# A gated scan with a mixture of experts: blank rows and row loads on all DMA rings, late jobs in whole tiles and rests, and new durations in the planner

## The chip, the core and the metric

The kernel runs on one core of a Trainium2 chip. A core has a matrix engine (PE; its weight loads are listed apart as PEld), a vector engine (DVE), an activation engine (ACT), POOL and SP, and 16 DMA engines that all queues share. Here SP issues the plain DMAs and POOL the indexed ones. The metric is the device time of one execution in microseconds; the median of three runs before the change is 884.57 us.

## The reference

Two stages, in float32. First a gated scan along each of four sequences of 3648 steps with 256 channels, then a mixture of 4 x 4 experts on the 14592 rows that come out:

```python
sig = 1.0 / (1.0 + np.exp(-f_logit))
f = lower_bound + (1.0 - lower_bound) * sig
for t in range(S):
    h = f[:, t] * h + (1 - f[:, t]) * x[:, t]
    y[:, t] = h
...
g_idx = argmax(y @ w_group)              # a group of four experts for each row
e_idx = argmax(y @ w_expert[g_idx])      # one expert in the group
out[row] = g_w * e_w * (np.maximum(y[row] @ w1[g, e], 0.0) @ w2[g, e])
```

`g_w` and `e_w` are the softmax weights of the chosen group and expert. An expert has a 256 x 1024 and a 1024 x 256 matrix.

## The kernel before, in words

**Front.** The rows are handled in 29 units of 512 (the last is half a unit), two units to a group. For a unit SP loads gates and inputs (`zt`, 1 MB, four buffers), ACT computes the gate (L352, L357), DVE the inflow and the scan of both channel halves (L362, L378). PE turns the result back to rows (L386) and computes the router's logits in four column groups (L401). For a group DVE finds each row's expert and its place in that expert's region of a scratch tensor `xs` in memory (the lines from L431 to L505), and POOL scatters the rows there, 128 to a DMA (L520).

**Expert jobs.** An expert's rows are worked off in two jobs. Its early job (kind A) takes the first n x 128 rows as soon as a certain unit is routed: `EARLY` has (unit, n) for each expert. When all rows are routed, DVE sorts the experts by what is left (`order`), and the late jobs (kind B) take the sorted experts one by one, with room for `CAPS[s]` rows at rank s. What fits no room would go through a loop at the end; with the data at hand it has no turn, before and after the change. Since an early job may start with fewer rows than it takes, each expert's region is preceded by rows that are blank, with an index that sends their result nowhere; a common block of blank rows serves jobs that have to be skipped. `blanks` (L322) writes them.

**A job.** SP loads four quarters of an expert's weights (`st`, 512 KB each, five buffers, L706) and the rows (`xr`, up to 256 rows to a piece, six buffers, L691). ACT rounds weights to float16 (L711), DVE puts the remainder in bfloat16 (L714). PE turns the rows (L732), ACT and DVE split them in the same way (L744, L748). The first product (L770 to L772, three partial products) has the weights as the stationary side and a chunk of two or three tiles of rows as the moving side; ACT applies the maximum with 0 (L787), DVE takes the remainder (L791). The second product (L803 to L805) has a tile's hidden rows as the stationary side and moves 256 columns of weights, 24 products to a tile; ACT scales the result (L816), and POOL scatters it to the output (L821). Three halves of PSUM banks take the second product's results in turn.

**The order.** `Plan` is a list scheduler that runs when the kernel is built. Each piece of work has an engine, a duration, what it depends on, the buffers it takes and a due time; a DMA has a size and goes through a model of shared bandwidth. The planner plays the program through with these numbers and writes out one fixed order for each engine. On the chip an engine runs its list in order and waits by semaphores. So a duration in the table changes the order of instructions, not the instructions. The due times are laid out from `BEGIN`, the time at which the first job is put.

Of the kernel before, what the change touches and what calls it, by code (L numbers as in the profile page):

```python
# [14 lines left out]
I32 = mybir.dt.int32  # L15
# [31 lines left out]
class Plan:  # L47
# [23 lines left out]
    def order(self):  # L71
# [44 lines left out]
        def rates():  # L116
            act = [e for e, q in queues.items() if q]
            return {e: min(380.0, 400.0 / len(act)) for e in act}

        def advance(now):  # L120
            left = now - clock[0]
            clock[0] = now
            for e, r in rates().items():
                b = left * r
                q = queues[e]
                while q and b > 0:
                    g = min(b, q[0][1])
                    q[0][1] -= g
                    b -= g
                    if q[0][1] <= 1e-3:  # L130
                        push(now + 900.0, finish, q.popleft()[0])
# [60 lines left out]
def gated_scan_moe(ctx: ExitStack, tc, zx, lower, wroute, wexp, out, S):  # L192
# [9 lines left out]
    BLK = P * max(t for t, _ in CAPS + [(n, P) for _, n in EARLY])  # L202
# [76 lines left out]
    for s in range(NE):  # L279
        V.memset(caps[:, s:s + 1], float(CAPS[s][0] * CAPS[s][1]))  # L280
# [41 lines left out]
    def blanks():  # L322
        b = rt.tile([P, 4, RW], F32, name="rows", bufs=ROW_BUFS)
        k = 4
        b = b.bitcast(I32)
        nc.gpsimd.memset(b, 0)
        nc.gpsimd.memset(b[:, :, D:D + 1], N)
        b = b.rearrange("p k c -> p (k c)")
        for r in range(0, BLK, P * k):
            n = min(P, (BLK - r) // k)  # L330
            sync.dma_start(out=xs_v[NT][r:r + n * k, :].rearrange("(p k) c -> p (k c)", k=k), in_=b[0:n])
        for q in range(0, NE, k):
            at = xs_v[NT + 1][FIRST - P + q * PITCH:FIRST - P + q * PITCH + 1, :]
            sync.dma_start(out=bass.AP(at.tensor, at.offset, [[PITCH * RW, k], [k * RW, P // k], [1, k * RW]]), in_=b)
# [308 lines left out]
    def make_job(kind, idx):  # L643
        j = Job()
        j.kind, j.idx = kind, idx
        j.tiles, j.w = (EARLY[idx][1], P) if kind == "A" else CAPS[idx] if kind == "B" else (1, P)
# [7 lines left out]
        j.pieces = [(c + t, min(2, m - t)) for c, m in j.chunks for t in range(0, m, 2)]  # L654
        j.cols = []
        for _, m in j.chunks:
            n = UNIT // (m * j.w)
# [18 lines left out]
    def piece_mask(j, pi):  # L676
        t0, m = j.pieces[pi]
        mk = j.mask[pi] = mo.tile([P, 2], I32, name="mk", bufs=16)
        if j.kind == "B":
            V.tensor_scalar(out=mk[:, 0:m], in0=rowno[m], scalar1=float(t0 * j.w),  # L680
# [4 lines left out]
    def job_rows(j):  # L685
        job_e(j)
        word = j.pos if j.kind == "A" else regs["pordi"][0:1, j.idx:j.idx + 1] if j.kind == "B" else regs["tabs"][0:1, 1:2]
        pos = sync.value_load(word, min_val=0, max_val=LROWS - j.tiles * j.w)
        for pi, (t0, m) in enumerate(j.pieces):
            r = j.rows[pi] = mo.tile([P, 2, RW], I32, name="xr", bufs=XR_BUFS)  # L690
            ld = sync.dma_start(out=r[0:j.w, 0:m],  # L691
                                in_=xs[bass.ds(pos + t0 * j.w, m * j.w), :].rearrange("(p k) c -> p k c", k=m))
# [26 lines left out]
    def x_turn(j, pi):  # L719
# [9 lines left out]
        p = j.w  # L729
# [5 lines left out]
    def x_views(j, pi):  # L735
        t0, m = j.pieces[pi]
        ch = chunk_of(j, t0)
        lo, w = (t0 - j.chunks[ch][0]) * j.w, m * j.w
# [35 lines left out]
    def m1_views(j, ch, cs):  # L774
        w = j.chunks[ch][1] * j.w
# [17 lines left out]
    def m2_mm(j, ch, t):  # L793
        p = j.w
        pm = j.pm[ch, t, "y"] = y_slot()
        ts = slice(t * p, (t + 1) * p)
        for c in range(KF):
            if j.full:
                nc.tensor.matmul(pm[0:p], j.hh[ch][:, c, ts], j.wh[2 + c // 4][:, (c % 4) * D:(c % 4 + 1) * D],
                                 start=(c == 0), stop=(c == KF - 1))  # L800
                continue
            wh, wl = (q[2 + c // 4][:, (c % 4) * D:(c % 4 + 1) * D] for q in (j.wh, j.wl))
            nc.tensor.matmul(pm[0:p], j.hh[ch][:, c, ts], wh, start=(c == 0), stop=False)  # L803
            nc.tensor.matmul(pm[0:p], j.hh[ch][:, c, ts], wl, start=False, stop=False)  # L804
            nc.tensor.matmul(pm[0:p], j.hl[ch][:, c, ts], wh, start=False, stop=(c == KF - 1))  # L805
# [6 lines left out]
    def m2_scale(j, ch, t):  # L812
        p = j.w
# [3 lines left out]

    def m2_out(j, ch, t):
        p = j.w
# [10 lines left out]
    def m1_ns(j, ch):  # L830
        return KF * KD * (4 if j.full else 3) * (j.chunks[ch][1] * j.w / 2.4 + 2.4)

    def m2_ns(j):
        return KF * (4 if j.full else 3) * 109.0
# [3 lines left out]
    for j in jobs:  # L838
        j.s1, j.s2 = {}, {}
        for ch in range(len(j.chunks)):  # L840
# [4 lines left out]
            if tail is not None:  # L845
                tj, tch = tail
                for t in range(tj.chunks[tch][1]):
                    tj.s2[tch, t] = clock
                    clock += m2_ns(tj)
            tail = (j, ch)  # L850
    tj, tch = tail
    for t in range(tj.chunks[tch][1]):
        tj.s2[tch, t] = clock
        clock += m2_ns(tj)

    want = {}
# [22 lines left out]
    for g, G in groups.items():  # L879
# [4 lines left out]
        for u in G["units"]:  # L884
            w = unit_range(u)[1] - unit_range(u)[0]
            q = w / 512.0
            k0 = key - 9000.0
# [16 lines left out]
            else:  # L904
                ld = A("SP", 340, lambda u=u: load_unit(u), key=k0 - 6000.0, new=[zt], size=int(1050000 * q))
# [13 lines left out]
            r = A("PE", 460, lambda u=u: router(u), after=sc, key=k0 + 1000, use=[hb], new=[("p", u, "r")])  # L919
# [4 lines left out]
        k1 = key - 6000.0  # L924
        rr, lg = ("rt", g), ("Lg", g)
        mx = A("DVE", 100 + 440 * frac, lambda g=g: route_max(g), after=lgs, key=k1, use=[lg], new=[rr])
        ex = A("ACT", 90 + 140 * frac, lambda g=g: route_exp(g), after=[mx], key=k1 + 100, use=[rr])
        fi = A("DVE", 150 + 600 * frac, lambda g=g: route_first(g), after=[mx], key=k1 + 200, use=[rr])
        ct = A("DVE", 150 + 480 * frac, lambda g=g: route_count(g), after=[fi], key=k1 + 300, use=[rr])
# [6 lines left out]
        ix = A("DVE", 100 + 520 * frac, lambda g=g: route_index(g), after=[pl], key=k1 + 600, use=[rr])  # L936
        tk = A("ACT", 130, lambda g=g: route_token(g), after=[mx], key=k1 + 150, use=[rr])
        wt = A("DVE", 250 + 380 * frac, lambda g=g: route_weight(g), after=[ex, fi, tk], key=k1 + 700, use=[rr])
# [3 lines left out]
        if g in close_at:  # L942
            T1[g] = A("DVE", 300 * len(runs(close_at[g])), lambda g=g: close(g), after=[tot], key=k1 + 800)
            ends[g] = [T1[g]]
        sct = [A("POOL", 1280, lambda g=g, t=t: scatter(g, t), after=[ix, pays[t // 4], copies[t // 2]], key=key - 4000.0 + t,
                 use=[rr, ("rows", G["units"][t // 4])], size=135000) for t in range(T)]
# [3 lines left out]
    tables = A("DVE", 2500, leftovers, after=[put], key=jobs[-13].at)  # L950
    regs["left"] = None

    for n, j in enumerate(jobs):
        base = j.at
        dep = [T1[member[EARLY[j.idx][0]]]] if j.kind == "A" else [put]
        rows_dep = dep + groups[member[EARLY[j.idx][0]] if j.kind == "A" else last]["scattered"]
# [4 lines left out]
        for i in range(4):  # L961
            d = base - 3000.0 + 700.0 * i if i < 2 else j.s2[0, 0] - 4000.0 + 1300.0 * (i - 2)
            ld = A("SP", 370, lambda j=j, i=i: job_weights(j, i), after=wdep, key=d - 9000.0,
# [8 lines left out]
        ld = A("SP", 500 + 370 * np_, lambda j=j: job_rows(j), after=rows_dep, key=base - 9500.0, new=xr, size=int(265000 * j.tiles * j.w / 256))  # L972
# [118 lines left out]
```

## Time and profile before

| what | value |
|---|---|
| median of 3 runs | 884.57 us (882.73 to 887.25) |
| the profiled execution's own time | 880.72 us |
| its span | 879.0 us |
| mean granted PE clock | 0.965 |
| PE / DVE / ACT / POOL busy | 753.7 / 537.3 / 463.5 / 294.2 us |
| moved by DMA | 146.89 MB |

An engine's busy time says how long instructions of it were in work; what sets the end is read from the idle time of the engine that is nearly always busy, and from what ended it. A row of a wait reads: who waited, for whom, how many microseconds in total, how often, the longest. A row of a stretch has its bounds, its length, and for PE, PEld, DVE, ACT and POOL the busy time and the number of instructions, then the granted PE clock, the mean busy share of the DMA engines, and GB/s.

### The profile page before, as it was taken

Reading aid. Unit: us, or ns where it says so; the run is one execution under the profiler, and the core shown is the slowest. Engines: PE = TensorE matmul, PEld = TensorE weight load, DVE = VectorE, ACT = ScalarE, POOL = GpSimd, SP = SyncE. Lnnn points to the kernel's source line nnn. Section 1 sums busy time; section 2 is a strip of 40 time slices with the busy share of each in tenths; the row PEclk is TensorE's granted clock in tenths of the full one; section 3 lists DMA queues with packets and bytes.
Section 4 is the critical chain, followed back from the end, with each engine's and each line's share of the span. In section 5 each row is a group of like instructions: output and inputs, shape, how many; then the busy total and the mean of one; then the engine's idle time right before and its main releaser. Section 6 shows DMA issues by size and latency. Waiting matters only on the chain.

```text
span 879.0 us, 17343 instructions
## 1 busy us (share of the span) xinstructions
PE 753.7 (86%) x6667; PEld 646.3 (74%) x6667; DVE 537.3 (61%) x1067; ACT 463.5 (53%) x852; POOL 294.2 (33%) x255
## 2 busy tenths in 40 slices
PE   3513499879897998998997698999999999999995
PEld 2312287767586787786886587999889989999894
DVE  6917999888895975753458452553654534655460
ACT  6506788666775764453434352543554544545551
POOL 0553726175425435515122121322321312222121
PEclk9999699988999999999999799999999999999998
DMA  7595888778856654314007641423543434443320
GB/s 288 168 326 208 298 326 297 251 232 303 277 202 220 211 188 150 123 59 141 23 31 234 215 117 46 158 73 111 156 143 103 122 105 136 144 153 122 108 95 19
DMA packets 48192, 146.89 MB, mean 167 GB/s; under 512 B 10707, under 2 KB 12958, under 8 KB 44652
## 3 DMA queue, kind: packets, MB, share of 16 engines
q1 hardware_dynamic: 33579, 115.67, 40.3%
q0 software_dynamic: 14240, 30.06, 10.0%
q8 instruction: 53, 0.87, 0.4%
q14 instruction: 32, 0.25, 0.1%
q10 hardware_dynamic: 288, 0.03, 0.0%
HBM read 112.65 MB, written 33.60 MB: 166 GB/s over the span
## 4 chain that ended last, share of the span: by engine, by line
PE 64%; DVE 8%; DMA 7%; issue 5%; ACT 2%; POOL 1%; another core or an unknown queue 1%; POOLq 0%; DVEq 0%; ACTq 0%
PE ps_y L803 10%; PE ps_y L805 10%; PE ps_y L804 10%; PE ps_m L770 10%; PE ps_m L772 10%; PE ps_m L771 10%; DMA st<-in_wexp_dram 4%; DMA xr<-xs 2%; DVE w L714 2%; PE ps_p L386 2%; DVE hh L791 2%; PE ps_p L732 2%; PE ps_p L401 1%; POOL out_dram L821 1%; ACT w L711 1%
## 5 line engine op out<-in xcount | busy, mean ns | idle before, releaser
L821 POOL DMA_INDIRECT out_dram<-o,meta x123 | 149.1, 1212 | 447.3 <-ACT o L816 412.2
L803 PE MATMUL ps_y<-w,hh 128*128 128x256 f16 (+6 forms) x984 | 269.9, 274 | 11.8 <-ACT o L816 10.2
L805 PE MATMUL ps_y<-w,hh 128*128 128x256 f16 (+6 forms) x984 | 269.8, 274 | 0.6 <-issue 0.6
L804 PE MATMUL ps_y<-w,hh 128*128 128x256 bf16 (+6 forms) x984 | 269.8, 274 | 0.0
L770 PE MATMUL ps_m<-x,w 128*128 128x256 f16 (+12 forms) x896 | 252.4, 283 | 10.4 <-DVE hh L791 8.2
L771 PE MATMUL ps_m<-x,w 128*128 128x256 bf16 (+12 forms) x896 | 252.4, 283 | 8.0 <-DVE x L748 5.5
L772 PE MATMUL ps_m<-x,w 128*128 128x256 f16 (+12 forms) x896 | 252.2, 282 | 0.3 <-issue 0.3
L791 DVE SCALAR_TENSOR_TENSOR hh<-ps_m,hh 128x512 bf16<-128x512 f32 (+11 forms) x270 | 164.2, 620 | 134.3 <-ACT hh L787 120.1
L787 ACT ACTIVATE hh<-ps_m 128x512 f16<-128x512 f32 (+11 forms) x270 | 146.0, 546 | 125.2 <-PE ps_m L772 109.1
L714 DVE TENSOR_TENSOR w<-st,w 128x1024 bf16<-128x1024 f32 x128 | 154.0, 1218 | 77.1 <-ACT w L711 74.9
L520 POOL DMA_INDIRECT xs<-rows,posi x114 | 142.3, 1248 | 128.2 <-issue 39.5
L816 ACT ACTIVATE o<-ps_y,meta 128x256 f32<-128x256 f32 (+6 forms) x123 | 57.1, 473 | 193.7 <-PE ps_y L805 147.2
L711 ACT CAST w<-st 128x1024 f16<-128x1024 f32 x128 | 132.6, 1049 | 20.0 <-DMA st<-in_wexp_dram 20.0
L804 PEld LDWEIGHTS <-hh 128*128 128x128 f16 (+6 forms) x984 | 111.5, 113 | 18.6 <-issue 11.5
L803 PEld LDWEIGHTS <-hh 128*128 128x128 f16 (+6 forms) x984 | 111.5, 113 | 9.6 <-issue 2.3
L805 PEld LDWEIGHTS <-hh 128*128 128x128 bf16 (+6 forms) x984 | 111.5, 113 | 8.0 <-issue 1.1
L771 PEld LDWEIGHTS <-w 128*128 128x128 f16 x896 | 88.7, 99 | 30.1 <-issue 14.4
L772 PEld LDWEIGHTS <-w 128*128 128x128 bf16 x896 | 88.7, 99 | 27.4 <-issue 11.2
L770 PEld LDWEIGHTS <-w 128*128 128x128 f16 x896 | 88.8, 99 | 18.4 <-issue 3.4
L378 DVE TENSOR_TENSOR_SCAN h<-zt,h 128x512 f32<-128x512 f32 (+4 forms) x56 | 65.4, 1172 | 0.9 <-PE ps_p L386 0.9
L401 PE MATMUL ps_p<-h,wr 128*32 128x128 f32 x456 | 26.5, 337 | 40.5 <-DVE h L378 27.3
L748 DVE TENSOR_TENSOR x<-ps_p,x 128x512 bf16<-128x512 f32 (+9 forms) x68 | 39.7, 613 | 20.8 <-ACT x L744 20.7
(126 smaller groups left out, 508.0 us busy)
## 6 DMA issues: line engine op xcount, KB each, us to landing
st<-in_wexp_dram SPq DMA_DIRECT2D x128, 512.0 KB
zt<-in_zx_dram SPq DMA_DIRECT2D x27, 1024.0 KB
xr<-xs SPq DMA_DIRECT2D x31, 258.0 KB
xs<-rows SPq DMA_DIRECT2D x5, 516.0 KB
xr<-xs SPq DMA_DIRECT2D x8, 249.9 KB
out_dram<-o,meta POOLq DMA_INDIRECT x123
xs<-rows,posi POOLq DMA_INDIRECT x114
xr<-xs SPq DMA_DIRECT2D x6, 241.9 KB
```

The lines of the kernel that those rows point to most:

```text
L520: sc = nc.gpsimd.indirect_dma_start(out=xs_v[G["t0"] + t][:, :], out_offset=bass.IndirectOffsetOnAxis(ap=G["posi"][:, t:t + 1], axis=0), i ...
L711: nc.scalar.copy(j.wh[i], j.st[i])
L714: V.tensor_tensor(out=j.wl[i], in0=j.st[i], in1=j.wh[i], op=ALU.subtract)
L770: nc.tensor.matmul(po, wh, xh[:, k], start=(k == 0), stop=False)
L771: nc.tensor.matmul(po, wh, xl[:, k], start=False, stop=False)
L772: nc.tensor.matmul(po, wl, xh[:, k], start=False, stop=(k == KD - 1))
L787: nc.scalar.activation(hi, pv, AF.Relu)
L791: V.scalar_tensor_tensor(out=lo, in0=pv, scalar=0.0, in1=hi, op0=ALU.max, op1=ALU.subtract)
L803: nc.tensor.matmul(pm[0:p], j.hh[ch][:, c, ts], wh, start=(c == 0), stop=False)
L804: nc.tensor.matmul(pm[0:p], j.hh[ch][:, c, ts], wl, start=False, stop=False)
L805: nc.tensor.matmul(pm[0:p], j.hl[ch][:, c, ts], wh, start=False, stop=(c == KF - 1))
L821: last_out[0] = nc.gpsimd.indirect_dma_start(out=out_v[out_n[0]][:, :], out_offset=bass.IndirectOffsetOnAxis(ap=lt[0:p, r, 0:1], axis=0), ...
```

## The change

**Blanks.** One constant tile of 64 x 2 blank rows is filled once by POOL. The region leads are written for four experts in one DMA, the common block in pieces, all with an outer dimension of 64, and each just ahead of the early jobs that need it. Before, all were written in one step, planned at 25 us, and the DMA of four leads had an outer dimension of 4.

**Late jobs.** `CAPS` is now a number of rows, a multiple of 32. A job is cut into whole tiles of 128 rows and, where needed, a rest of 64 and a rest of 32. Before, a late job was n tiles of one width, 92 to 128 rows. A chunk of the first product may now be up to 384 rows of mixed tiles. For a rest the second product splits the hidden dimension in two or four parts, which go to column groups of 64 or 32 of the matrix engine and to different partitions of PSUM; ACT scales the first part and DVE adds the others (`m2_sum`).

**Numbers.** Two early jobs are smaller by one tile each, one of them starts a unit earlier. `BEGIN` goes from 55 to 85 us, weights may be loaded 16 us ahead instead of 20, the bandwidth is 340 GB/s in all, a landing takes 1.5 us, and many durations of the planner's table are replaced. The core of the diff:

```diff
-         (14, 3), (16, 4), (18, 4), (20, 4), (22, 5), (24, 5), (26, 6), (26, 6)]
-CAPS = [(7, 124), (6, 128), (6, 124), (5, 124), (5, 120), (5, 116), (5, 108), (4, 128),
-        (4, 120), (4, 120), (4, 116), (4, 108), (3, 128), (3, 104), (2, 92), (1, 128)]
+         (14, 3), (16, 4), (18, 4), (20, 4), (22, 4), (23, 5), (26, 6), (26, 5)]
+CAPS = [864, 768, 736, 608, 608, 576, 544, 512, 480, 480, 448, 448, 448, 416, 288, 128]
-BEGIN = 55.0
-BLANKS_AT = 25000.0
+BEGIN = 85.0
-AHEAD = 20000.0
+AHEAD = 16000.0
+RATE = 340.0
+LAND = 1500.0
+POOL_NS = 1400.0
...
-            return {e: min(380.0, 400.0 / len(act)) for e in act}
+            return {e: RATE / len(act) for e in act}
...
-        for q in range(0, NE, k):
-            at = xs_v[NT + 1][FIRST - P + q * PITCH:FIRST - P + q * PITCH + 1, :]
-            sync.dma_start(out=bass.AP(at.tensor, at.offset, [[PITCH * RW, k], [k * RW, P // k], [1, k * RW]]), in_=b)
+    def blank_common(r, n):
+        sync.dma_start(out=xs_v[NT][r:r + n * P, :].rearrange("(n p k) c -> p n (k c)", p=P // 2, k=2),
+                       in_=blank.rearrange("p k c -> p (k c)")[:, None, :].broadcast_to([P // 2, n, 2 * RW]))
+
+    def blank_leads(e, n):
+        at = xs_v[NT + 1][FIRST - P + e * PITCH:FIRST - P + e * PITCH + 1, :]
+        sync.dma_start(out=bass.AP(at.tensor, at.offset, [[2 * RW, P // 2], [PITCH * RW, n], [1, 2 * RW]]),
+                       in_=blank.rearrange("p k c -> p (k c)")[:, None, :].broadcast_to([P // 2, n, 2 * RW]))
...
+        j.tw = [P] * (j.cap // P)
+        for w in (64, 32):
+            if sum(j.tw) + w <= j.cap:
+                j.tw.append(w)
...
-            m = 3 if j.tiles - t == 3 else min(2, j.tiles - t)
+            m = j.tiles - t if sum(j.tw[t:]) <= 3 * P else 2
...
+        parts = P // p
+        n = KF // parts
+        for i in range(n):
...
+            for m in range(len(prods[0])):
+                for q in range(parts):
+                    c = q * n + i
+                    h, w = prods[q][m]
+                    nc.tensor.matmul(pm[q * p:(q + 1) * p], h[:, c, ts], w[2 + c // 4][:, (c % 4) * D:(c % 4 + 1) * D],
+                                     start=(i == 0 and m == 0), stop=(i == n - 1 and m == len(prods[0]) - 1),
+                                     **({"tile_position": (0, q * p)} if parts > 1 else {}))
...
+    def m2_sum(j, ch, t):
...
+        for q in range(1, P // p):
+            V.scalar_tensor_tensor(out=o[0:p], in0=j.pm[ch, t, "y"][q * p:(q + 1) * p], scalar=lt.bitcast(F32)[0:p, r, 1:2],
+                                   in1=o[0:p], op0=ALU.mult, op1=ALU.add)
...
-    def m2_ns(j):
-        return KF * (4 if j.full else 3) * 109.0
+    def m2_ns(j, ch, t):
+        return KF * (4 if j.full else 3) * 109.0 * j.tw[j.chunks[ch][0] + t] / P
...
-            r = A("PE", 460, lambda u=u: router(u), after=sc, key=k0 + 1000, use=[hb], new=[("p", u, "r")])
+            r = A("PE", 1050, lambda u=u: router(u), after=sc, key=k0 + 1000, use=[hb], new=[("p", u, "r")])
...
-    A("SP", 1100, blanks, after=[], key=0.0, new=[("rows", "blank")], size=3000000, wait=BLANKS_AT)
-    put = A("DVE", 4200, order, after=[tot, *T1.values()], key=need[last] - 3000.0, new=[("h", "order")])
+    put = A("DVE", 6000, order, after=[tot, *T1.values()], key=need[last] - 3000.0, new=[("h", "order")])
```

More of the change, by code (lines that the diff above doesn't have):

```diff
@@ L320, in unit_range, with blank_rows @@
         return u * UNIT, min(N, (u + 1) * UNIT)
[L322 to L331, printed above, removed]
-        for q in range(0, NE, k):
-            at = xs_v[NT + 1][FIRST - P + q * PITCH:FIRST - P + q * PITCH + 1, :]
-            sync.dma_start(out=bass.AP(at.tensor, at.offset, [[PITCH * RW, k], [k * RW, P // k], [1, k * RW]]), in_=b)
+    blank = const.tile([P // 2, 2, RW], I32, name="blank")
+    def blank_rows():
+        nc.gpsimd.memset(blank, 0)
+        nc.gpsimd.memset(blank[:, :, D:D + 1], N)
+    def blank_common(r, n):
[5 more added lines that the diff above has]
+                       in_=blank.rearrange("p k c -> p (k c)")[:, None, :].broadcast_to([P // 2, n, 2 * RW]))
     def load_unit(u, k=None):
@@ L650, in make_job @@
         while t < j.tiles:
[L651 removed]
+            m = j.tiles - t if sum(j.tw[t:]) <= 3 * P else 2
             j.chunks.append((t, m))
             t += m
[L654 removed]
+        j.cw = [j.to[t + m] - j.to[t] for t, m in j.chunks]
+        j.pieces = []
+        for c, m in j.chunks:
+            t = c
+            while t < c + m:
+                n = 2 if t + 1 < c + m and j.tw[t] == j.tw[t + 1] == P else 1
+                j.pieces.append((t, n))
+                t += n
         j.cols = []
[L656 to L657 removed]
+        for w in j.cw:
+            n = UNIT // w
             j.cols.append([list(range(c, min(KF, c + n))) for c in range(0, KF, n)])
@@ L942, in gated_scan_moe, with blanked @@
         if g in close_at:
-            T1[g] = A("DVE", 300 * len(runs(close_at[g])), lambda g=g: close(g), after=[tot], key=k1 + 800)
+            T1[g] = A("DVE", 390 * len(runs(close_at[g])), lambda g=g: close(g), after=[tot], key=k1 + 800)
             ends[g] = [T1[g]]
-        sct = [A("POOL", 1280, lambda g=g, t=t: scatter(g, t), after=[ix, pays[t // 4], copies[t // 2]], key=key - 4000.0 + t,
+        sct = [A("POOL", POOL_NS, lambda g=g, t=t: scatter(g, t), after=[ix, pays[t // 4], copies[t // 2]], key=key - L_SCATTER + t,
                  use=[rr, ("rows", G["units"][t // 4])], size=135000) for t in range(T)]
         G["scattered"] = (groups[g - 1]["scattered"] if g else []) + sct
-    A("SP", 1100, blanks, after=[], key=0.0, new=[("rows", "blank")], size=3000000, wait=BLANKS_AT)
-    put = A("DVE", 4200, order, after=[tot, *T1.values()], key=need[last] - 3000.0, new=[("h", "order")])
-    tables = A("DVE", 2500, leftovers, after=[put], key=jobs[-13].at)
+    made = A("POOL", 900, blank_rows, key=0.0, wait=3000.0)
+    late = need[last] - 25000.0
+    leads = {}
+    for q in range(0, NE, 4):
+        at = min([j.at for j in jobs if j.kind == "A" and q <= j.idx < q + 4] + [late])
+        leads[q] = A("SP", 340, lambda e=q: blank_leads(e, 4), after=[made], key=at - 17000.0, size=540000, wait=at - 30000.0)
+    commons = []
+    done = 0
+    for j in jobs:
+        n = j.tiles if j.kind == "A" else BLK // P
+        if n > done:
+            at = min(j.at, late)
+            commons.append((n, A("SP", 340, lambda a=done * P, n=n - done: blank_common(a, n), after=[made], key=at - 16500.0,
+                                 size=132000 * (n - done), wait=at - 30000.0)))
+            done = n
+    def blanked(j):
+        n = j.tiles if j.kind == "A" else BLK // P
+        return ([leads[j.idx // 4 * 4]] if j.kind == "A" else list(leads.values())) + [t for m, t in commons if m <= n]
+    put = A("DVE", 6000, order, after=[tot, *T1.values()], key=need[last] - 3000.0, new=[("h", "order")])
+    tables = A("DVE", 3500, leftovers, after=[put], key=jobs[-13].at)
     regs["left"] = None
```

123 lines of the change are left out of this document (71 added, 52 removed).

## The prediction

> **What bounds the kernel now.** I read the page's head first, then busy time in six stretches (the columns are the length, then PE, PEld, DVE, ACT and POOL busy, granted clock, DMA share and GB/s).
>
> ```profile
> span 879.0 us, 17343 instructions
> PE 753.7 (86%) x6667; PEld 646.3 (74%) x6667; DVE 537.3 (61%) x1067; ACT 463.5 (53%) x852; POOL 294.2 (33%) x255
> 0.00:109.00 109.00, 40.89 (x298) 26.01 (x299) 74.63 (x185) 61.11 (x115) 48.43 (x54) 0.92 0.73 257
> 109.00:340.00 231.00, 210.60 (x1899) 172.52 (x1899) 191.33 (x336) 159.51 (x292) 107.94 (x85) 0.96 0.72 246
> 340.00:473.00 133.00, 123.06 (x1073) 101.62 (x1072) 73.26 (x188) 56.76 (x119) 47.27 (x45) 0.99 0.30 96
> 473.00:543.00 70.00, 55.64 (x449) 47.05 (x449) 35.87 (x77) 28.80 (x48) 10.56 (x8) 0.90 0.51 156
> 543.00:863.00 320.00, 318.36 (x2907) 294.48 (x2906) 162.21 (x285) 156.01 (x277) 76.62 (x61) 1.00 0.39 119
> 863.00:879.00 16.00, 5.15 (x48) 4.61 (x45) 0.00 (x0) 1.30 (x3) 3.38 (x3) 0.80 0.07 18
> ```
>
> PE idles 68.1 us before the first expert product at 109, 20.4 in the next stretch, 9.9, then 14.4 where the late jobs begin, and only 1.6 in 543 to 863. So the end is PE's work plus those idle times: after 543 only less PE work helps, before it only shorter waits. Two waits stand out. The first, from the waits of 24 to 75 us and then SP's rows and the busy time in slices:
>
> ```profile
> DVE mx L431 <- ACT Lg L420: 25.1, 3, 24.2
> ACT zt L352 <- DMA zt<-in_zx_dram: 23.1, 2, 22.9
> PE ps_p L412 <- ACT rs L407: 20.9, 1, 20.9
> 30.67 8.81 SPq L334 DMA_DIRECT2D xs<-rows  x4
> 39.59 8.81 SPq L344 DMA_DIRECT2D zt<-in_zx_dram  x2
> 36.00:40.00 4.00, 1.69 (x15) 1.11 (x13) 3.69 (x7) 1.73 (x5) 3.39 (x3) 1.00 0.37 98
> 52.00:56.00 4.00, 0.00 (x0) 0.00 (x0) 0.00 (x0) 0.00 (x0) 2.92 (x3) 1.00 1.01 397
> ```
>
> Four blank stores go out at 30.7; while they run the DMA engines are 0.37 busy at 98 GB/s, against 397 GB/s later, and the next load of zx lands so late that ACT waits 22.9 us, DVE 24.2 behind it, PE 20.9 behind both. Nothing else works then: this is the whole front, stopped.
>
> The second wait, where the late jobs start (waits of 474 to 500, the row loads' own view, two slices):
>
> ```profile
> ACT w L711 <- DMA st<-in_wexp_dram: 11.8, 3, 11.2
> PE ps_y L803 <- ACT o L816: 9.7, 1, 9.7
> L691 SPq DMA_DIRECT2D xr<-xs x4: 255/262/331, 472.2 to 473.8; - x4
> L754 DVE COPY meta<-xr x4: 169/170/171, 480.0 to 489.1; 124x4 int32<-124x4 int32 x3, 124x2 int32<-124x2 int32 x1
> 484.00:488.00 4.00, 0.00 (x0) 0.00 (x0) 0.64 (x4) 0.00 (x0) 0.00 (x0) 0.84 0.70 192
> 488.00:492.00 4.00, 0.19 (x2) 0.13 (x2) 2.13 (x5) 1.66 (x3) 0.00 (x0) 0.50 0.26 104
> ```
>
> Four row loads of 124 rows are issued from 472.2 to 473.8 and used from 480.0 to 489.1; the weights queued behind them come 11.2 us late at ACT, whose queue holds the output scale that PE needs, 9.7 us. The clock falls to 0.50 meanwhile.
>
> **Front: the blanks.** SP's start before (zt is a unit of zx, rows the blank tile, st a quarter of weights):
>
> ```order
> L347 DMA zt<-in_zx_dram 128x512 x4
> L344 DMA zt<-in_zx_dram 128x2048 x6
> L331 DMA xs<-rows 128x1032
> L331 DMA xs<-rows 96x1032
> L334 DMA xs<-rows 4x32x1032 x4
> L344 DMA zt<-in_zx_dram 128x2048 x2
> L706 DMA st<-in_wexp_dram 128x1024 x2
> ```
>
> and in the change:
>
> ```order
> L360 DMA zt<-in_zx_dram 128x512 x4
> L357 DMA zt<-in_zx_dram 128x2048 x12
> L346 DMA xs<-blank 64x4x516
> L341 DMA xs<-blank 64x2x516
> L357 DMA zt<-in_zx_dram 128x2048
> L734 DMA st<-in_wexp_dram 128x1024 x2
> ```
>
> All 3.0 MB of blanks stood ahead of the seventh whole unit; now 0.8 MB stands behind twelve, the outer dimension of the lead store is 64 instead of 4, and the rest follows before the jobs that need it. The Trainium skill ("DMA: Bandwidth & Descriptors", "Why a DMA increments its semaphore by 16 and not by 1") says that a DMA uses the largest number of engines up to 16 that divides both sides' outer dimension; by that 4 of 16, at its 27 GiB/s each, would hold the leads' 2.1 MB for 18 us, an estimate. The trace agrees in size: 98 GB/s in that slice.
>
> With the stall gone DVE sets the front, since it was 74.6 us busy before 109 and its rows there are these:
>
> ```profile
> L378 DVE TENSOR_TENSOR_SCAN h<-zt,h 128x512 f32<-128x512 f32 x18 | 23.0, 1278 | 0.0
> L714 DVE TENSOR_TENSOR w<-st,w 128x1024 bf16<-128x1024 f32 x9 | 10.9, 1216 | 0.9 <-ACT w L711 0.6
> L459 DVE TENSOR_TENSOR_SCAN scn<-rmask,oh 128x128 bf16<-128x128 bf16 x4 | 1.7, 425 | 0.1
> ```
>
> Ahead of the first x split DVE now has four scans more (4 x 1.28 = 5.1), one routing group more (some 16 small rows, the scan of 0.43 the longest: about 4.5, and 0.5 to close it) and six weight splits fewer (6 x 1.22 = 7.3): +2.8. Idle there was 34.4, less the 24.2: 10.2. So 74.6 + 2.8 + 10.2 = 87.6; I take 88 in place of 109, **-21**. Bounds: 82 if half of the idle goes too, 96 if the row loads of the first job, which wait for POOL's scatters, come late. PE's router and transposes for two more units, about 3 us, are then done in idle time: **-3**, bounds 0 and -4. The rest of the early stage keeps its 20.4 us of idle: row loads there wait on SP for scatters and hold weights behind them. Units now lead their jobs by more, and DVE has 2.8 us less left, but splits moved behind the first product crowd a DVE already 83% busy. I take **-4**, bounds -15 and +10.
>
> **Late start: whole rows.** SP ahead of the first late job (xr is a piece of its rows), before:
>
> ```order
> L706 DMA st<-in_wexp_dram 128x1024
> L632 DMA tab<-resi 128x3
> L688 TENSOR_LOAD pordi
> L688 ISA x2
> L691 ISA
> L691 DMA xr<-xs 124x516
> L691 ISA
> L691 DMA xr<-xs 124x516
> ```
>
> and in the change:
>
> ```order
> L734 DMA st<-in_wexp_dram 128x1024
> L715 TENSOR_LOAD pordi
> L715 ISA x2
> L719 ISA
> L719 DMA xr<-xs 128x516
> L719 ISA
> L719 DMA xr<-xs 128x516
> ```
>
> 124 rows divide among 4 engines by the rule above, 128 among 16. The loads come one table store earlier; what was 9.1 us from first to last landing I price by the 397 GB/s slice (0.9 MB, 2.3 us plus what is queued). Of the stretch's 14.4 us of idle and about 5 us of lowered clock (0.90 over 55.6 busy) I take **-12**, bounds 0 and -18, because the sort that picks the jobs and the loads behind it have no more PE work to hide under than before, when the sort began at 458.5 and PE ran dry at 482:
>
> ```profile
> 458.54 0.17 DVE end L555
> 480.00:484.00 4.00, 2.13 (x20) 1.76 (x18) 0.32 (x2) 0.00 (x0) 0.00 (x0) 1.00 0.88 252
> ```
>
> **Rests: column groups.** The 68 late tiles of 92 to 128 rows become 58 whole ones, ten of 64 and nine of 32 rows; early tiles go from 55 to 53. A rest on PE (ps_y is the output, w a quarter of weights, hh the hidden rows):
>
> ```order
> L839 MATMUL ps_y_167<-w_6096,hh 32x256
> L839 LDWEIGHTS hh
> L839 MATMUL ps_y_167<-w_6096,hh 32x256
> L839 LDWEIGHTS hh
> L839 MATMUL ps_y_167<-w_6103,hh 32x256
> L839 LDWEIGHTS hh
> L839 MATMUL ps_y_167<-w_6103,hh 32x256
> ```
>
> Still 24 pairs of load and product, but four in a row go to different columns. Before, a tile's products, the router's column groups and plain transposes cost:
>
> ```profile
> 119.28 0.27 PE L803 MATMUL ps_y<-w,hh 128*128 128x256 f16 x1
> 121.79 0.27 PE L805 MATMUL ps_y<-w,hh 128*128 128x256 f16 x1
> 303.98 0.57 PE ps_p L401 x16
> 314.05 0.44 PE ps_p L386 x4
> ```
>
> The first two rows are the first and last product of one tile's 24, 2.51 us and 23 steps of 0.109 apart: a tile is 2.62 us, 123 tiles 322 us. If groups overlap fully, 111 x 2.62 + 10 x 1.31 + 9 x 0.65 = 309.4: -12.4. The router's 16 records of 32 columns take 0.57 us, 36 ns each, where a transpose takes 110: 3.1 times, so rests at 0.84 and 1.69 us make it -7. I take **-8**, near that row, since it has the change of grouping in it. Without overlap 19 rests cost as much as whole tiles, 7 tiles more: +18. First products keep their columns, 15136 rows both times.
>
> **What is added.** 37 sums on DVE of 256 columns; the nearest row is twice as wide:
>
> ```profile
> L791 DVE SCALAR_TENSOR_TENSOR hh<-ps_m,hh 128x512 bf16<-128x512 f32 (+11 forms) x270 | 164.2, 620 | 134.3 <-ACT hh L787 120.1
> ```
>
> So about 0.35 each, 13 us, and 7 scales, 7 output scatters and 14 row loads: hidden in 543 to 863, where DVE is half busy and POOL a quarter; **+1**, bounds 0 and +8 if the sums hold the three output slots. The last job is the same tile as before, so the tail stays.
>
> **Sum.** -21 -3 -4 -12 -8 +1 = -47, from the profiled execution's 880.7 (span 879.0): 833.7. The median of the runs shown is 884.57, 3.9 above the profiled one; I forecast **837**.
>
> **Rivals.**
> *Groups don't overlap.* The Trainium skill ("TensorEngine Tiling (Array Packing)", "Restrictions and Gotchas") excludes fast weight load from column tiling. As a mechanism here: if a load can't hide, each pair costs the router's load row,
>
> ```profile
> L401 PEld LDWEIGHTS ps_p<-h,wr x456: 106/110/177, 7.7 to 405.7; 128*32 128x32 f32 x152
> ```
>
> 110 ns, 24 of them 2.6 us, a rest as dear as a tile: +18 instead of -8, 863. Against it: the same row's pairs came every 36 ns, though in f32. 8%.
> *The front's gain is given back.* Early jobs start sooner on a DVE that was 191 of 231 us busy; if DVE, not PE, sets 109 to 340, the 21 us shrink to the DVE work saved there, about 5: 853. For it: the 20.4 us of idle; against it, the splits are the same in number. 15%.
> *The rings stay narrow.* If 64 and 128 rows don't spread, the late start keeps its 14 us, the front loses 5: 854. 7%.
> *Slower: row loads block SP.* Six row buffers held the pieces of 2.5 late jobs and hold those of 1.8 now (38 row loads for 16 jobs, then 52). SP waits in order, weights behind. This was there before:
>
> ```profile
> SPq L691 <- PE ps_p L732: 75.1, 16, 10.7
> ```
>
> It costs PE nothing until a wait passes the weights' lead; from 3.3 us for each of 16 late jobs (53 us) the kernel is slower, and 4 us give about 901. Against it: 1.6 us of PE idle in 320 with 16 such waits. 7%.
>
> **How the numbers follow.** Forecast 63%, rivals 8, 15, 7 and 7. The forecast's own range is 816 to 856 from its bounds taken together; with the first three rivals 812 to 864 holds over 8 in 10. Half a per cent (4 us) is what a measurement of this kernel tells from no change: faster 0.90, within 0.03, slower 0.07.
>
> **What would show it.** The first expert product at 82 to 96 us with no ACT wait over 8 us on zx before it; the late start's PE idle under 5 us; a 32-row rest under 0.9 us and a 64-row rest under 1.7; PE still without gaps afterwards. The forecast is wrong if the first product comes after 96, if PE idles over 30 us between it and the late start, or if rests cost 2.6 us.

## The result, and the profile after

The changed kernel takes 838.93 us (median of 4 runs, 836.23 to 844.35) and the kernel before, beside it, 883.65 us (4 runs, 879.36 to 887.25). The ratio is 0.950, with a 95% interval of 0.944 to 0.957. The forecast was 837, with a range of 812 to 864. The profiled execution took 836.23 us with a span of 834.2.

Busy time of the changed kernel in stretches that answer to those shown of before (columns as there; the last begins where the last outputs are stored):

```profile
0.00:88.00 88.00, 47.86 (x356) 30.48 (x357) 77.99 (x202) 63.16 (x125) 51.46 (x54) 0.85 0.81 279
88.00:440.00 352.00, 320.74 (x2801) 262.48 (x2800) 252.26 (x470) 207.70 (x388) 149.75 (x127) 0.95 0.62 208
440.00:500.00 60.00, 58.87 (x497) 48.74 (x496) 40.58 (x107) 32.01 (x57) 14.12 (x10) 1.00 0.50 153
500.00:820.00 320.00, 319.10 (x3165) 278.38 (x3163) 185.95 (x377) 161.15 (x297) 77.11 (x69) 1.00 0.39 124
820.00:834.20 14.20, 6.99 (x88) 5.77 (x85) 2.73 (x5) 2.50 (x5) 2.83 (x3) 0.85 0.09 29
```

Length less PE's busy time is PE's idle time:

| stretch | before | after | change |
|---|---|---|---|
| to the first expert product | 68.1 | 40.1 | -28.0 |
| early stage (109 to 473; 88 to 440) | 30.3 | 31.3 | +0.9 |
| late start (473 to 543; 440 to 500) | 14.4 | 1.1 | -13.2 |
| late stage | 1.6 | 0.9 | -0.7 |
| end | 10.9 | 7.2 | -3.6 |
| PE busy in all | 753.7 | 753.6 | -0.1 |

The table says where the 44.8 us of span came from: the front and the late start, and 3.6 us at the end. It also shows two things that don't fit a simple story. The early stage idles as long as before, and PE is busy as long as before although the rests should have taken work off it. The kernels run again, below, take up both.

The front's marks, from the timeline and the waits of the first 100 us:

```profile
86.25 0.42 PE L797 MATMUL ps_m<-x,w 128*128 128x256 f16 x1
ACT zt L365 <- DMA zt<-in_zx_dram: 6.9, 4, 2.2
```

The first expert product starts at 86.25 instead of 107.97, and the wait of 22.9 us on zx is gone (longest now 2.2). The rests, as PE's line of the second product (PE, then PEld) in the time of one 64-row rest and of the 32-row rest behind it, each up to the start of the next work's first product, and the sums on DVE by shape:

```profile
568.36:569.79 1.43, 1.43 (x24) 1.23 (x24) 1.00 0.08 23
569.79:570.56 0.77, 0.77 (x26) 0.55 (x24) 1.00 0.47 69
L859 DVE SCALAR_TENSOR_TENSOR o<-ps_y,meta,o 32x256 f32<-32x256 f32 x27 | 12.9, 479 | 8.6 <-ACT o L852 8.0
L859 DVE SCALAR_TENSOR_TENSOR o<-ps_y,meta,o 64x256 f32<-64x256 f32 x10 | 4.8, 485 | 16.3 <-ACT o L852 16.3
```

A 64-row rest takes 1.43 us and a 32-row rest 0.77, within 0.01 for each of the ten and nine in this trace; half and a quarter of a whole tile's 2.62 would be 1.31 and 0.65. (The second row counts 26 products because the last two of the rest before are still in work.) The groups overlap fully: a rest's 24 products start within 1.23 and 0.57 us. What is over, about 0.12 us for each rest, lies behind its last product: the next work follows after 0.20 us, where a whole tile's products follow each other after 0.109.

### The profile page after: what moved, and what is told of

Read it like the earlier page. It is cut to its first block, busy times and chain, and to the rows that moved or that the text cites. A ratio compares the mean times of both kernels' runs of the same rounds, so it can differ in the third digit from the quotient of the medians.

```text
span 834.2 us, 18026 instructions
## 1 busy us (share of the span) xinstructions
PE 753.6 (90%) x6897; PEld 625.8 (75%) x6897; DVE 559.5 (67%) x1157; ACT 466.5 (56%) x871; POOL 295.3 (35%) x262
## 4 chain that ended last, share of the span: by engine, by line
PE 63%; issue 14%; DVE 8%; DMA 5%; POOL 5%; ACT 4%; another core or an unknown queue 0%; SPq 0%; POOLq 0%; DVEq 0%; ACTq 0%
PE ps_y L839 29%; PE ps_m L797 10%; PE ps_m L799 10%; PE ps_m L798 9%; POOL out_dram L865 3%; PE ps_p L760 2%; DMA xs<-rows,posi 2%; DVE h L391 2%; DVE w L742 2%; POOL xs L533 2%; DMA zt<-in_zx_dram 2%; PE ps_p L399 2%; DVE hh L818 1%; ACT w L739 1%; ACT o L852 1%
## 5 line engine op out<-in xcount | busy, mean ns | idle before, releaser
L839 PE MATMUL ps_y<-w,hh 128*128 128x256 f16 (+4 forms) x3120 | 334.9, 275 | 10.1 <-issue 8.7
L839 PEld LDWEIGHTS <-hh 128*128 128x128 f16 (+4 forms) x3120 | 277.2, 99 | 52.4 <-issue 19.2
L797 PE MATMUL ps_m<-x,w 128*128 128x256 f16 (+8 forms) x912 | 254.5, 280 | 12.2 <-DVE hh L818 8.5
L798 PE MATMUL ps_m<-x,w 128*128 128x256 bf16 (+8 forms) x912 | 254.3, 280 | 6.0 <-DVE x L776 6.0
L818 DVE SCALAR_TENSOR_TENSOR hh<-ps_m,hh 128x512 bf16<-128x512 f32 (+5 forms) x269 | 163.3, 622 | 137.8 <-ACT hh L814 96.9
L799 PE MATMUL ps_m<-x,w 128*128 128x256 f16 (+8 forms) x912 | 254.3, 280 | 0.1
L814 ACT ACTIVATE hh<-ps_m 128x512 f16<-128x512 f32 (+5 forms) x269 | 145.1, 546 | 138.5 <-PE ps_m L799 107.3
L852 ACT ACTIVATE o<-ps_y,meta 128x256 f32<-128x256 f32 (+2 forms) x130 | 60.9, 472 | 178.0 <-PE ps_y L839 139.1
L798 PEld LDWEIGHTS <-w 128*128 128x128 f16 x912 | 90.4, 99 | 31.3 <-issue 16.1
L776 DVE TENSOR_TENSOR x<-ps_p,x 128x512 bf16<-128x512 f32 (+2 forms) x81 | 41.2, 541 | 35.7 <-ACT x L772 31.4
L370 ACT ACTIVATE zt<-zt,mid,half 128x512 f32<-128x512 f32 (+1 forms) x58 | 45.7, 813 | 0.3
L399 PE MATMUL ps_p<-ident,h 128*128 128x128 f32 x228 | 42.0, 342 | 0.0
```

The costliest lines, as they stand in the source:

```text
L797: nc.tensor.matmul(po, wh, xh[:, k], start=(k == 0), stop=False)
L798: nc.tensor.matmul(po, wh, xl[:, k], start=False, stop=False)
L799: nc.tensor.matmul(po, wl, xh[:, k], start=False, stop=(k == KD - 1))
L814: nc.scalar.activation(hi, pv, AF.Relu)
L818: V.scalar_tensor_tensor(out=lo, in0=pv, scalar=0.0, in1=hi, op0=ALU.max, op1=ALU.subtract)
L839: nc.tensor.matmul(pm[q * p:(q + 1) * p], h[:, c, ts], w[2 + c // 4][:, (c % 4) * D:(c % 4 + 1) * D], start=(i == 0 and m == 0), stop=(i = ...
```

## The experiments

The experiments ran on three chips, and the kernel before beside them took 870.29 us (f1, l1, l2, e1), 870.17 (a0, r1, n1, p1) and 867.78 (b0, s1, p2, p3), some 13 to 16 us less than in the first timing. So the changed kernel (a0) and the kernel before (b0) were run there too, and all prices but f1's are against a0. Only n1, p1 and r1 ran on a0's chip; the others' prices compare two chips, on which the kernel before differs by 0.1 us (f1, l1, l2, e1) or 2.4 (s1, p2, p3). All medians below are of 4 runs. Whether another chip or another hour made the difference to the first timing isn't known; the expectations speak of the chip of the experiments as if it were one. Those of f1, l1, l2 and e1 give times on the scale of the first timing (883.65 and 838.93), so that only their differences can be compared. Where they say that a stretch loses time, they mean its length less its products counted at their undisturbed steps (0.109 us for 256 columns), so idle time and slowed work together.

| kernel | us | ratio to the kernel before (95%) | against the changed kernel |
|---|---|---|---|
| a0: changed kernel | 805.65 | 0.926 (0.925 to 0.928) | |
| n1: narrow leads, new places | 813.09 | 0.935 (0.934 to 0.937) | +7.4 |
| p1: old numbers of the plan | 824.35 | 0.947 (0.946 to 0.949) | +18.7 |
| p2: begin at 55 | 819.96 | 0.943 (0.939 to 0.948) | +14.3 |
| p3: begin at 100 | 820.95 | 0.945 (0.941 to 0.949) | +15.3 |
| s1: old tiles | 827.17 | 0.952 (0.948 to 0.956) | +21.5 |
| r1: rests without groups | 835.79 | 0.960 (0.958 to 0.962) | +30.1 |
| l1: late loads as 124 and 4 rows | 813.10 | 0.934 (0.931 to 0.938) | +7.5 |
| l2: late loads as 112 and 16 rows | 808.26 | 0.929 (0.925 to 0.933) | +2.6 |
| e1: early residuals left out | 800.37 | 0.919 (0.915 to 0.923) | -5.3 |
| f1: before, wide leads | 853.13 | 0.980 (0.976 to 0.984) | (-17.2 against before) |

### Width of the blank stores: f1 and n1

```
 # f1, in the kernel before
-[[PITCH * RW, k], [k * RW, P // k], [1, k * RW]]), in_=b)
+[[2 * RW, P // 2], [PITCH * RW, k], [1, 2 * RW]]),
+    in_=b[0:P // 2, None, 0:2 * RW].broadcast_to([P // 2, k, 2 * RW]))
 # n1, in the changed kernel
-[[2 * RW, P // 2], [PITCH * RW, n], [1, 2 * RW]]
+[[PITCH * RW, n], [2 * RW, P // 2], [1, 2 * RW]]
```

> The kernel before with one thing changed: the four lead stores are written with 64 rows of two as outer dimension instead of 4 blocks; place, bytes and order stay. Theory (the width stops the front): 3.0 MB at the 397 GB/s of a later slice take 7.6 us, the stall of 22.9 us on zx goes, the first expert product comes at 88 to 95 instead of 108, and the time falls by what the early stage leaves of it, 864 to 872 us. Rival A (the place, not the width: the blanks stand ahead of the seventh unit): first product after 103, 878 to 886. Rival B (the early stage gives all of the front's gain back): first product before 95, but 880 to 886.

> The changed kernel with the four lead stores written with 4 as outer dimension again, at their new places behind twelve units and ahead of the jobs that need them. With the kernel before, the wide stores at the old place and the changed kernel this makes a square of width and place. Theory (width matters where stores stand ahead of work that waits; the places now hide them): 540 KB at the 98 GB/s of the old stores are 5.5 us each, one ahead of the first weights, three more in the early stage: 2 to 8 us over the changed kernel. Rival (the place alone was the gain): 0 to 2 us.

f1's first product and its wait on zx in the first 100 us:

```profile
90.37 0.27 PE L771 MATMUL ps_m<-x,w 128*128 128x256 f16 x1
ACT zt L353 <- DMA zt<-in_zx_dram: 11.4, 5, 5.4
```

With the same bytes at the same place the longest wait falls from 22 us (b0) to 5.4, the first product comes at 90.4 instead of 107.3, and the kernel takes 0.980 of the time. So the form of the store makes this stall, and 17 us of front came out as 17 us of time: the rival that the early stage gives it all back falls. f1 also writes runs of two rows instead of four, but n1 swaps the two outer dimensions and nothing else: the narrow form at the new places is 7.4 us dearer than the changed kernel, with the first product at 89.6, 3.1 later than its twin's. So it is the outer dimension, and the new places hide part of what the narrow form costs. Both came out as the theory had it (f1 by its difference, 17.2 in a forecast of 12 to 20). What is left of the front, DVE sets, as these two stretches of the changed kernel (a0) show, in which it is busy 53.3 of 56 us:

```profile
30.00:60.00 30.00, 19.23 (x141) 12.22 (x139) 28.30 (x64) 22.70 (x49) 20.43 (x16) 1.00 0.78 258
60.00:86.00 26.00, 14.31 (x107) 9.17 (x108) 24.99 (x54) 18.56 (x37) 21.73 (x15) 1.00 0.88 304
```

### The changed kernel and the kernel before, run again: a0 and b0

Nothing is edited.

> The changed kernel itself, on the chip of the experiments. The twins with two issues for each late load took 0.929 and 0.934 of the kernel before there, the change 0.950 where it was timed first. Theory (the chips differ in how long the early stage loses TensorE time, and a second issue costs nothing or a little): 0.925 to 0.930 of the kernel before. Rival (two smaller loads land sooner than one of 128 rows): 0.947 to 0.953.

> The kernel before, for its profile on the chip of the experiments. Where the change was timed first, PE waited 11 to 12 us for nothing that the profile shows, 18 times before and 25 times after, and no run of the experiments has such a wait; theory (that is the chip, not the kernel): none here either, and the early stage from the first product to the late start loses 28 to 38 us instead of 47. Rival (the change's order brings or takes these waits): 10 us or more of them here.

The change takes 0.926 of the time here, not 0.950, and both theories on this held: it is not the split loads, and the waits without a shown cause are in neither kernel here; the kernel before takes 338 us from its first product to the sort instead of 349, so that it loses some 36 us there instead of 47. Busy time of the kernel before (four rows) and of the changed kernel (four rows), cut at the first product and at the start of the sort that picks the late jobs:

```profile
0.00:109.00 109.00, 40.53 (x304) 25.87 (x305) 75.27 (x185) 61.68 (x115) 47.87 (x54) 0.75 0.73 261
109.00:447.00 338.00, 314.18 (x2858) 261.03 (x2857) 250.46 (x464) 210.37 (x401) 146.85 (x121) 0.98 0.57 196
447.00:543.00 96.00, 79.50 (x662) 68.81 (x660) 51.15 (x137) 38.80 (x64) 22.21 (x20) 0.93 0.47 144
543.00:867.50 324.50, 312.29 (x2851) 288.30 (x2848) 160.18 (x283) 153.43 (x274) 76.77 (x62) 0.99 0.38 118
```

```profile
0.00:88.00 88.00, 48.75 (x355) 31.31 (x356) 78.26 (x202) 63.34 (x125) 51.59 (x53) 1.00 0.80 277
88.00:399.00 311.00, 295.67 (x2718) 248.35 (x2717) 241.71 (x441) 203.14 (x380) 147.21 (x122) 0.99 0.65 225
399.00:500.00 101.00, 99.02 (x888) 83.98 (x886) 64.34 (x166) 48.87 (x86) 25.39 (x25) 1.00 0.50 164
500.00:803.50 303.50, 295.38 (x2942) 257.06 (x2940) 173.80 (x350) 151.02 (x280) 72.03 (x65) 1.00 0.37 119
```

PE's idle time falls by 29.2 in the front (68.47 to 39.25), 8.5 in the early stage (23.8 to 15.3), 14.5 at the late start (16.5 to 2.0) and 4.1 behind it, and its busy time by 7.7: 64 us in all. So the early stage does gain, and PE does get less work, where nothing else disturbs. The changed kernel's execution in the first timing was 30.7 us longer than this one, that of the kernel before 11.5.

What disturbed it, in the changed kernel's first trace: PE's waits in the whole span, and 8 us of its timeline in which 23 of one whole tile's 24 products start:

```profile
PE ps_y L839 <- issue: 8.7, 18, 0.9
...
PE ps_m L797 <- issue: 3.5, 7, 0.8
```

```profile
343.87 1.75 PE L839 MATMUL ps_y<-w,hh 128*128 128x256 f16 x10 [0.21 <-ACT hh L814]
346.06 0.61 PE L839 MATMUL ps_y<-w,hh 128*128 128x256 bf16 x4 [0.44 <-issue]
347.49 0.38 PE L839 MATMUL ps_y<-w,hh 128*128 128x256 f16 x2 [0.81 <-issue]
348.21 0.27 PE L839 MATMUL ps_y<-w,hh 128*128 128x256 bf16 x1 [0.34 <-issue]
348.94 0.60 PE L839 MATMUL ps_y<-w,hh 128*128 128x256 f16 x2 [0.46 <-issue]
350.34 1.01 PE L839 MATMUL ps_y<-w,hh 128*128 128x256 bf16 x4 [0.81 <-issue]
```

"issue" is a wait for nothing that the profile shows. Its operands are there, yet after the first ten the products come in ones to fours, some 0.7 to 1.4 us apart, and the tile takes over 7 us instead of 2.62. Such waits stand 25 times between 94 and 434 in this trace (12.2 us), 18 times between 109 and 468 in the first trace of the kernel before (11.3 us), and in none of the twelve traces of the experiments between 80 and 500. The granted clock falls with it, as the slice at its end shows:

```profile
350.00:352.00 2.00, 1.66 (x8) 1.41 (x8) 0.00 (x0) 0.66 (x3) 0.00 (x0) 0.50 1.07 324
```

In that slice 8 products take 1.66 us, 0.21 each instead of 0.109. So a lower clock makes busy time longer: the changed kernel's PE was busy 14.7 us longer than in a0 (753.55 against 738.82), that of the kernel before 7.2, so the rests' saving didn't show in the sum of the first timing. What makes PE wait so stays open. It isn't the change by itself, since the same program lacks it in a0; and the queue that brings instructions moved 54 packets (0.88 MB) in both executions.

### The plan's numbers: p1, p2 and p3

```
 # p1 (with RATE and the durations of the diff as before, too)
-BEGIN = 85.0
+BEGIN = 55.0
-AHEAD = 16000.0
+AHEAD = 20000.0
-LAND = 1500.0
-POOL_NS = 1400.0
+LAND = 900.0
+POOL_NS = 1280.0
 # p2
-BEGIN = 85.0
+BEGIN = 55.0
 # p3
-BEGIN = 85.0
+BEGIN = 100.0
```

> The changed kernel with the planner's old durations, rates and lead times (start of the products at 55 us, stores and scatters shorter, loads faster); work, tiles and blank stores as changed. The order differs from the start: the first leads behind six whole units instead of twelve, the first weights behind eight instead of thirteen. Theory (the numbers move only what is hidden): within 6 us of the changed kernel, first expert product within 5 us of 86. Rival (the numbers carry the late start or the front, by what is loaded ahead of what): 10 us or more over it.

> The changed kernel with one number of the plan changed back: the products are taken to begin at 55 us instead of 85, so that the scans' due times spread otherwise and fewer units stand ahead of the first weights. All old numbers together cost 18.7 us. Theory (it is this number: units done before the first product are work that the crowded early stage doesn't have): 13 to 20 us over the changed kernel. Rival (it is the durations, rates and lead times): 6 us or less over it.

> The changed kernel with the start of the products in the plan at 100 us instead of 85. Theory (more units ahead empty the early stage further than they delay the first product): first product at 90 to 96, 797 to 804 us on this chip. Rival (DVE sets the front, each unit more delays it by as much as it saves later): 806 to 815 us.

My theory for p1 fell: the numbers carry 18.7 us, and one of them, the time at which the products are taken to begin, 14.3. Busy time from 88 to 440 of the changed kernel (a0), p1, p2 and p3, in this order:

```profile
88.00:440.00 352.00, 334.69 (x3048) 280.71 (x3047) 275.23 (x541) 225.36 (x417) 159.32 (x133) 1.00 0.65 223
```

```profile
88.00:440.00 352.00, 325.56 (x2942) 269.38 (x2941) 272.13 (x540) 220.71 (x417) 154.23 (x131) 0.98 0.63 215
```

```profile
88.00:440.00 352.00, 327.21 (x2947) 271.11 (x2948) 270.80 (x538) 220.73 (x413) 154.88 (x131) 0.98 0.63 213
```

```profile
88.00:440.00 352.00, 327.47 (x2920) 271.56 (x2921) 274.09 (x541) 224.69 (x409) 157.34 (x131) 0.97 0.66 229
```

p1's first product comes at 86.3 and p2's at 87.9, about as early as the changed kernel's 86.5. They lose it in two places: PE does 46.64 - 39.25 = 7.4 (p1) and 6.0 us (p2) less in the front's idle time, since fewer units have gone by, and it does 9.1 and 7.5 us less between 88 and 440. More units ahead aren't better without end: p3's first product comes at 98.6, and PE also waits once more for rows, 5.1 us:

```profile
PE ps_p L760 <- DMA xr<-xs: 5.4, 2, 5.1
```

So 85 beat both 55 and 100; p3 came out still dearer than its rival had it (806 to 815), and both its theories fall. Each changes one number and keeps those that were set beside 85; whether 55 or 100 would do better with the others set anew wasn't tried.

### Rests: r1

```
-        parts = P // p
+        parts = 1
...
-        for q in range(1, P // p):
+        for q in range(1, 1):
```

> The changed kernel in its own order, but the rests' second products run as whole tiles do: 24 products one after the other in the same columns, and no sums on DVE. Theory (groups overlap, PE sets the end after 440): 19 rests at 2.62 instead of 10 at 1.31 and 9 at 0.90 make 49.8 - 21.2 = 28.6 us more than the changed kernel. Rival (what the rests save on PE is lost again to the sums or to the waits around them): 10 us or less.

30.1 us more, against 28.6 expected (which put 0.13 us of each 64-row rest to the 32-row one; 10 x 1.43 + 9 x 0.77 make the same 21.2): the theory holds, and what the rests save on PE is saved in time. Nothing takes it back: PE's only waits from 500 to 800 in the changed kernel (a0) are these two, although the 37 sums cost DVE 17.7 us.

```profile
PE ps_y L839 <- ACT o L852: 0.3, 2, 0.2
PE ps_m L797 <- DVE hh L818: 0.3, 1, 0.3
```

### The late start: l1, l2 and s1

```
 # l1: cut = 124, l2: cut = 112, for late pieces of 128 rows; s1: EARLY and CAPS of before
-            ld = sync.dma_start(out=r[0:p, 0:m], in_=xs[... m * p ...])
+            for a, b in ((0, cut), (cut, p)):
+                ld = sync.dma_start(out=r[a:b, 0:m], in_=xs[... m * (b - a) ...])
```

> The changed kernel, with each late load of 128-row pieces issued as two, 124 rows and 4 rows, so that both parts have an outer dimension that 16 doesn't divide. Theory (the narrow row loads made the late start dear): the weights behind them come late again, 848 to 858 us, with 8 to 15 us of PE idle at the late start. Rival (the late start gained by the order of the work around it, not by the loads): within 4 us of its twin with 112 and 16 rows, PE idle there under 4.

> The twin of the kernel with 124 and 4 rows: the same number of loads, but of 112 and 16 rows, both multiples of 16. It prices the second issue alone, some 0.4 us of SP for each load: 838 to 843 us by both theories.

> The changed kernel with the tiling of before: early jobs of 55 tiles, late jobs in equal tiles of 92 to 128 rows, so no rests and no column groups, and row loads of 124, 120, 116, 108, 104 and 92 rows; blanks and the planner's numbers stay as changed. Theory (the tiling is worth the rests' 9 us and the 5 us that 124 and 4 rows cost over 112 and 16): 13 to 18 us over the changed kernel. Rival (the late start's whole 17.7 us hang on these loads): 25 us or more over it, with PE idle over 8 us at the late start.

l1 costs 4.8 us more than its twin, hardly more than the rival's 4, and 7.5 more than a0, where the theory had 9 to 19. From 400 to 440 PE idles 5.4 us in l1, 3.2 in l2 and 2.0 in a0. s1, with the whole tiling undone, costs 21.5: between theory (13 to 18) and rival (25). Its PE idle from the sort's start (407.5) to 500 is 13.6. The rows tell why the two differ. First the kernel before (b0): SP's table store, row loads and weights behind the sort (which begins at 447.6), and the times when DVE takes the first three pieces:

```profile
459.50 0.35 SPq L632 DMA_DIRECT2D tab<-resi  x1
460.92 1.87 SPq L691 DMA_DIRECT2D xr<-xs  x4
463.05 16.70 SPq L706 DMA_DIRECT2D st<-in_wexp_dram  x5
...
468.77 0.15 DVE L754 COPY meta<-xr 124x4 int32<-124x4 int32 x1
472.56 0.17 DVE L754 COPY meta<-xr 124x4 int32<-124x4 int32 x1 [3.44 <-DMA xr<-xs]
476.02 0.17 DVE L754 COPY meta<-xr 124x4 int32<-124x4 int32 x1 [3.10 <-DMA xr<-xs]
```

and the changed kernel (a0; sort from 398.5):

```profile
409.46 3.88 SPq L719 DMA_DIRECT2D xr<-xs  x5
414.32 0.36 SPq L645 DMA_DIRECT2D tab<-resi  x1
415.66 3.35 SPq L734 DMA_DIRECT2D st<-in_wexp_dram  x3
...
421.02 0.16 DVE L782 COPY meta<-xr 128x4 int32<-128x4 int32 x1
421.89 0.16 DVE L782 COPY meta<-xr 128x4 int32<-128x4 int32 x1
422.62 0.16 DVE L782 COPY meta<-xr 128x4 int32<-128x4 int32 x1
```

DVE takes the pieces of the narrow loads 3.8 and 3.5 us apart, waiting for each landing; the wide ones don't make it wait, and the third piece is used 24.1 us after the sort's start instead of 28.4. But the loads also leave 11.0 us after the sort's start instead of 13.3, because the table store, which waits for the end of DVE's work on the leftovers, is no longer ahead of them. l1 has the loads ahead of the store and undoes the width alone; s1 has the store at 419.8 and its loads from 421.2, 13.7 us after the sort's start, and undoes both. Its weights come late once more, ACT waits and PE behind it (waits of 407 to 500):

```profile
PE ps_m L794 <- ACT x L769: 7.3, 1, 7.3
```

The execution of s1 that was profiled is its fastest (822.73, 4.4 under the median) and spans 17.4 us more than a0's: 11.6 are PE idle at the late start, 3.0 idle elsewhere, and only 2.8 busy time (741.6 against 738.8), although the rests save more on the second products, whose rows in s1 and a0 are these:

```profile
L836 PE MATMUL ps_y<-w,hh 128*128 128x256 f16 (+11 forms) x2952 | 336.1, 273 | 0.7 <-ACT o L849 0.2
L839 PE MATMUL ps_y<-w,hh 128*128 128x256 f16 (+4 forms) x3120 | 327.4, 273 | 0.6 <-ACT o L852 0.3
```

Of these 8.7 us a0's smaller pieces take most back: 14 more transposes of rows (260 against 246, that line busy 37.8 us against 33.6) and 48 more first products. So against the old tiles the rests are worth less on PE than r1 suggests (30.1 less 18.3 for seven tiles fewer, 11.8). The place of the store wasn't tried alone.

### DVE in the early stage: e1

```
 def job_lo(j, i):
+    if j.kind == "A":
+        return
```

(and the early jobs' residual names the main half, so the products are as many.)

> The changed kernel without the residual of the early jobs' weights: the 64 splits of 1.22 us on DVE are left out for them (78 us of DVE before 440), and the products that read the residual read the main half again, as many and as long as before, so the output isn't the reference's. Order and everything else stay. Theory (a crowded DVE is what costs the early stage its 54 us without PE work between 88 and 440): PE idle there falls from 31 to under 16 and the time to 810 to 825. Rival (it is the clock, the supply of instructions and the row loads behind the scatters): PE idle stays over 24, 832 to 841.

Its times are to be read against a0: 5.3 us less, and 14.2 us of PE idle between 88 and 440 instead of 17.3. The theory falls: 14.2 is under the 16 that it had named, but without the edit the idle is 17.3 here and not the 31 of the first timing, so only 3 us of it went. 78 us of splits left out (DVE busy 60.6 us less between 88 and 440) are worth 5. PE's waits from 88 to 440, in a0 and in e1:

```profile
PE ps_m L797 <- DVE hh L818: 7.1, 8, 1.5
PE ps_m L798 <- DVE x L776: 4.3, 5, 1.2
```

```profile
PE ps_m L801 <- DVE hh L822: 3.6, 4, 1.6
PE ps_m L802 <- DVE x L780: 3.3, 5, 1.4
```

They are short waits for one step of DVE each, and more than half of them stay when a fifth of its work there is gone: a chain that PE catches up with, not a DVE that is full.

## Why the prediction was right, and where it wasn't

**Front (-21, and -3 for units done in idle time): the -21 right, the -3 too small.** The first product came at 86.25 (forecast 88, bounds 82 to 96), 21.7 us earlier, with no wait on zx over 2.2. PE's idle fell by 28.0, some 6 of it by more work of the front on PE (busy 47.9 us before 88, 40.9 before 109), where the step had 3. f1 and n1 show the cause given, the outer dimension; DVE sets what is left, as assumed. By the ring rule of the Trainium skill ("DMA: Bandwidth & Descriptors", "Why a DMA increments its semaphore by 16 and not by 1") the wide form should have done this by itself, and the trace agrees: the longest zx wait is 5.4 us at the old place.

**Early stage (-4, "keeps its idle"): wrong in size, and hidden by something else.** The step weighed the units done ahead as some 7 us, here and in the -3. p1 puts the plan's numbers at 18.7 and p2 the one that sets how many go ahead at 14.3. In the first timing none of it was seen: idle rose by 0.9, with 12 us of waits without a shown cause in it, and the lowered clock behind them. The kernel before had 11.3 us of such waits there too, yet from its first product to the sort it idled only 4.2 us more than in b0 (28.0 against 23.8), the changed kernel 12.9 more than in a0 (28.2 against 15.3); why like waits cost the two so unlike amounts isn't shown. That the sum came out, -47 forecast and -44.7 measured, is in part luck: an undervalued gain and an unforeseen loss of like size. On the chip of the experiments the same sum from 870 gives 823, and the kernel took 805.65.

**Late start (-12, bounds 0 and -18): right in mechanism, a little past the far bound in size.** Idle fell by 13.2, and the lowered clock (0.90 over 55.6 us busy) went too, some 5.6. The step named the width and the store's place. l1 against its twin gives the width alone 4.8 us; the larger part needs the store's place or the order of the work around it as well, which weren't tried apart.

**Rests (-8) and what is added (+1): the groups right, PE's saving in all smaller.** 64-row rests took 1.43 and 32-row ones 0.77, under the 1.7 and 0.9 that were to show it and nearer to full overlap (1.31 and 0.65) than to the router's rate (1.69 and 0.84). With them the second products take 312 us instead of 322, -10 where the step had -8. But "first products keep their columns" left out that smaller pieces bring more transposes and more first products: all of PE's busy time differs by 2.8 us between s1 and a0, and by 7.7 between b0 and a0, at a mean clock of 0.949 and 0.997. A sum costs 0.48 us, not 0.35, and is hidden. The tail, which was to stay, lost 3.6 us of idle; no run shows why.

**Rivals.** Groups without overlap: excluded by the rests' times and r1; the Trainium skill's sentence that column tiling excludes fast weight load ("TensorEngine Tiling (Array Packing)", "Restrictions and Gotchas") costs nothing that shows here, as 24 loads of 64 columns take 1.23 us, no longer than the starts of their products. Narrow rings: excluded by f1. Front given back: not in a0, where early idle fell by 8.5. Row loads blocking SP: the wait grew as feared, from b0 to a0,

```profile
SPq L691 <- PE ps_p L732: 74.6, 16, 10.7
```

```profile
SPq L719 <- PE ps_p L760: 102.9, 16, 12.2
```

but the weights' lead covers 12 us, and PE waits 0.6 us from 500 to 800.

## What to carry to other kernels

A transfer's outer dimension deserves a look wherever other work queues behind it: the same 2.1 MB cost 17 us more in one form than in the other. A planner's single number (when the products begin) was worth 14 us against a value 30 us earlier and 15 against one 15 us later, more than the durations around it; price such a number by the work it moves into idle time, and try it on both sides. And a trace can hold losses that belong to neither kernel: run both kernels again before a term that "didn't come" is explained away.

## What was not expected of the hardware

PE's waits without a shown cause, 0.2 to 0.9 us each in the changed kernel, in both kernels' first traces and in none of the later ones, with the clock at 0.50 in the one looked at. Of the 30.7 us by which the changed kernel's first execution is longer than the later one, 16 are idle time (12.2 of them these waits) and 14.7 longer busy time; the cause is open. And column groups overlap fully in both widths, but each rest pays about 0.12 us at its end: the next work follows its last product after 0.20 us instead of 0.109, so that a quarter of a tile's products take 0.77 us and not 0.65.
